# The end of a two-layer decode kernel: order of the closing products, the row layout of w_down, and the form of the last projection

## Chip, cores and metric

The kernel runs on one core of one Trainium2 chip. The metric is the time of one execution on the device in microseconds (us); the median of three runs of the kernel before is 651.43 us (650.32 to 651.67). One execution was recorded by the hardware profiler; all views below come from it.

## What is computed

Four sequences (B = 4) each take one decode step through two identical layers. A layer is a grouped-query attention block over a cache of 8192 positions, and then a gated feed-forward block, each with a layer norm ahead and a residual sum behind. Both layers use the same weights and the same caches. All arrays are bf16.

```python
def _A_ref(x, k_cache, v_cache, wq, wo):      # x (4,1,512); caches (4,8,8192,128)
    q = (x @ wq) ...                          # 32 query heads of 128, 4 for each of 8 cache heads
    scores = einsum(q, k) * 128 ** -0.5
    o = einsum(softmax(scores), v)
    return o.reshape(B, 1, 4096) @ wo

def _B_ref(x, w_gate, w_up, w_down):          # 512 -> 1792 -> 512
    return (silu(x @ w_gate) * (x @ w_up)) @ w_down

x = A_x
x = x + _A_ref(layernorm(x), ...);  x = x + _B_ref(layernorm(x), ...)
x = x + _A_ref(layernorm(x), ...);  x = x + _B_ref(layernorm(x), ...)
```

## The kernel before

**Units and slots.** The attention of a layer is cut into 16 units: a unit is one sequence and a pair of cache heads (its K is 4 MB, its V is 4 MB). Unit u belongs to head pair u // 4 and sequence u % 4. Layer 0 takes the units in the order 0 to 15; layer 1 takes 15, 14, 13 (which it partly finds still in SBUF) and then 0 to 12, so that unit 12 is the last. K and V go into four slots of SBUF and a fifth one that first held wq. The list `cmds` holds all transfers in order; `pump` issues the next one on the SP queue as soon as the pieces of the slot that it needs have been given back by `freed`. The V of a layer's last unit is loaded in three parts (blocks 0 to 3, 4 and 5, 6 and 7). The slot of an earlier K then takes the feed-forward weights: w_gate, the part of w_up that is not kept from layer 0, and w_down (`load_weight`, `load_wd`). The last part of w_down lies where the transposed probabilities of the last unit stood (`late_pT`), so it is issued only when those are used up.

**One unit.** `keys` transposes K on DVE (`turn`, L480) and multiplies it with the query on PE (`scores`, L504). Then come the steps of the softmax: `max_p` and `max_t` find the maximum, `exps` subtracts it and takes the exponential on ACT (L526, L529, L531, L533), `total` sums with a product with ones on PE and a reciprocal on DVE (L549, L552), and `turn_p` transposes the probabilities on DVE (L545). `values` multiplies them with V on PE in four parts (`products`, L604, in groups of four matmuls that write to four 32-row groups of the same bank), `gather` adds up eight or four sub-blocks on DVE (L656, L659), `combine` multiplies with a selection matrix on PE (L664) and scales with the reciprocal of the total (L666). When all four sequences of a head pair are done, `mix` reorders the result (L681, L684) and `project` multiplies it with a quarter of wo (L693).

**The order of the work** is written by hand. `blocks` is a list of PE blocks with an assumed time of 0.9 us each. `line` is a list of small steps with a gap, a tag and a function; `advance` takes the time of each block off the first step's gap and issues steps that are due. `flush(tag)` issues all steps up to the last one with that tag. Ahead of the second last unit's products (unit 11 in layer 1) all steps tagged with the last unit are flushed, that is also its exponential, total and transpose. In part 2 of the last unit (`part(2)`, L620 to L626) the steps left in the line except a projection are issued first, then the products of the second half of the positions on the first two blocks, then the gather of those; part 3 has the products on the other two blocks, the projection that was held back, the other half of the gather, and combine.

**The feed-forward block** (`ffn`, L760 to L808). `center` computes x minus its mean; 56 products with w_gate and 56 with w_up (L776, weights stationary, four columns moving) follow, with the norm's deviation in the middle of the first 56 (L725, L727, L729). L783 to L790 form silu(gate) * up, `hT`. Then 56 products with w_down (L795) in four parts. Row f of w_down must lie in the same partition as value f of hT. For a part of e rows per partition the row is a * 128 + p * e + (fo - a), so that gate and up weights are read at a step of e elements: four for fo = 0 to 11 and two for fo = 12 and 13. In layer 1 the sum with x goes to `xoT` (L805), four transposes (L849) in two pairs turn it, DVE and ACT copy one pair each to SBUF (L855, L857), and SP sends the result out (L859). The copy on DVE is recorded as a write of all names in `PB`, of which `xoT` is one.

The parts of w_down before:

```python
WD = ((0, 4), (4, 8), (8, 12), (12, 14))
```

Of the kernel before, what the change touches and what calls it, by code (L numbers as in the profile page):

```python
# [103 lines left out]
def bass_interleave_layers__gqa_block_cached__swiglu_ffn__decode_kernel(  # L104
# [40 lines left out]
    with ExitStack() as es:  # L145
# [11 lines left out]
        wq_sb = kv[:, QS, :].rearrange("p (k f) -> p k f", k=KT)  # L157
        WQ = [f"wq{i}" for i in range(2)]
        wo_sb = sb("wo_sb", [P, Hq, D], BF16)
        WD = ((0, 4), (4, 8), (8, 12), (12, 14))  # L160

        W_SLOT = (1, 3)
        O_WU = KT * F
# [5 lines left out]
            o = k // 2 * 2 * P + k % 2  # L169
            return slice(o, o + 2 * P - 1, 2)  # L170

        def columns(o, e=2):
            return kvf[:, o:o + e * (P - 1) + 1:e]

        def wg_at(s, k, f, e):
            return columns(s * SL + k * F + f, e)

        def wu_at(s, k, f, e):
            o = k * F + f
            return columns((NSLOT + 1) * SL + o if o < RES else s * SL + O_WU + o - RES, e)  # L180

        def wd_at(s, fo, k):
            return columns(s * SL + O_WD + fo * D + pick2(k).start)
# [37 lines left out]
        u0 += 3 * B  # L221
        xx, xc = (pbf[:, u0 + i * XB:u0 + (i + 1) * XB] for i in range(2))
        u0 += 2 * XB
        xoT = pb[:, 2 * u0:2 * u0 + XB]
        assert 2 * u0 + XB <= SW and SW >= D
        xio = pb[0:B, 0:D]
        PB = ["pb", "gr", "eg", "gw", "hT", "xs", "vs", "lnv", "xx", "xc", "xoT"]

        GP = G // 2
        RJ = [NA] * (GP - 1) + [2]  # L230
# [23 lines left out]
        def place(role, a, b, rows=slice(0, P)):  # L254
            k, o = (ONE, ROLE[role][1]) if held[0] else (ROLE[role][0], 0)
            assert o + b <= BANKF
            return bank(k)[rows, o + a:o + b], f"pb{k}"

        sem = lambda name: es.enter_context(nc.semaphore(name))
        engines = {"pe": nc.tensor, "act": nc.scalar, "dve": nc.vector, "pool": nc.gpsimd, "sp": nc.sync}  # L260
# [130 lines left out]

        def load_wd(w0, j, also=()):
            a, b = WD[j]
            T.dma("sp", w0[:, O_WD + a * D:O_WD + b * D],
                  B_w_down[a * P:b * P, :].rearrange("(p e) n -> p (e n)", e=b - a), sem_w["wd"][j],
                  writes=[f"wd{j}"] + list(also))

        def pump():
# [168 lines left out]
        def keys(L, u, before, lag):  # L567
            def block(q):
                if q == 0:
                    place_q(L, u)  # L570
                scores(L, u, q)
                finished(K(L, u), q, q + 1)
                if q == NB - 1:
                    step = lambda gap, fn: [gap, u, lambda: fn(u)]
                    line.extend([step(0.0, max_p), step(1.2, max_t)])
                    (line if before is None else behind.setdefault(before, [])).extend(
                        [step(0.9, exps), step(1.0, total), step(0.3, lambda u: turn_p(L, u))])

# [9 lines left out]
        def values(L, u):  # L588
# [21 lines left out]
            def part(i):  # L610
                if i == 0:
                    flush(order[L][-1] if u == order[L][-2] else u)
                h = i // 2
                ts = range(i % 2 * (TB // 2), (i % 2 + 1) * (TB // 2))
                if not last:
                    products(h, 0, QH, ts)
                elif not h:
                    products(h, 0, QH // 2, ts)
                    products(h, QH // 2, QH, ts)
                elif i == 2:  # L620
                    while line and line[0][1] != "proj":
                        line.pop(0)[2]()
                    for step in line:
                        step[0] = 99.0
                    products(h, 0, QH // 2, range(TB))
                    gather(0, QH // 2)  # L626
                else:
                    products(h, QH // 2, QH, range(TB))
                if i % 2:
                    finished(V(L, u), h * QH, (h + 1) * QH)  # L630
                if i == 3:
                    if p_name == "late":
                        freed(W_SLOT[L], NB, NB + 1)
# [126 lines left out]
        def ffn(L):  # L760
# [8 lines left out]
            for at, wname, bk in ((wg_at, "wg", gb), (wu_at, "wu", ub)):  # L769
                for fo in range(FO):  # L770
                    if bk == gb and fo == FO // 2:
                        deviation(zero_sb, "zero")
                    a, b = next(w for w in WD if w[0] <= fo < w[1])
                    f = a * P + fo - a
                    for kt in range(KT):
                        T.op("pe", lambda e: e.matmul(bank(bk)[:, fo * B:(fo + 1) * B],  # L776
                                                      lhsT=at(s, kt, f, b - a),
                                                      rhs=xn[:, kt * B:(kt + 1) * B],
                                                      start=(kt == 0), stop=(kt == KT - 1)),
                             reads=rooms[wname] + names[wname] + ["xn"], writes=[f"pb{bk}"],  # L780
                             sig=(fo == FO - 1 and kt == KT - 1))
                freed(s, *((0, 3) if wname == "wg" else (3, 4)))
# [5 lines left out]
            T.op("dve", lambda e: e.reciprocal(eg, eg), reads=["eg"], writes=["eg"])  # L788
            T.op("dve", lambda e: e.tensor_tensor(eg, gw, eg, ALU.mult), reads=["gw", "eg"], writes=["eg"])
            T.op("dve", lambda e: e.tensor_tensor(hT, eg, uT, ALU.mult), reads=[f"pb{ub}", "eg"], writes=["hT"])  # L790
            for j, (a, b) in enumerate(WD):
                k = OBK[0] if j else SBK[1]
                for nt in range(KT):
                    for fo in range(a, b):
                        T.op("pe", lambda e: e.matmul(bank(k)[:, nt * B:(nt + 1) * B],  # L795
                                                      lhsT=wd_at(s, fo, nt),
                                                      rhs=hT[:, fo * B:(fo + 1) * B],
                                                      start=(j < 2 and nt == 0 and fo == a),
                                                      stop=(j in (0, len(WD) - 1) and nt == KT - 1 and fo == b - 1)),
                             reads=["hT", f"wd{j}"] + rooms["wd"], writes=[f"pb{k}"], sig=(fo == b - 1))  # L800
                if not j:
                    add_to_x(bank(k)[:, 0:XB], f"pb{k}")
            freed(s, 4, NB)
            if L == 1:
                T.op("dve", lambda e: e.tensor_tensor(xoT, xT[:], bank(k)[:, 0:XB], ALU.add),  # L805
                     reads=["x", f"pb{k}"], writes=["xoT"])
            else:
                add_to_x(bank(k)[:, 0:XB], f"pb{k}")  # L808


        load_weight("wq", 0)
# [30 lines left out]
            ffn(L)  # L842
        assert issued[0] == len(cmds)

        for c, (k, eng) in enumerate(((LNB, "dve"), (OUTB, "act"))):
            ob = bank_bf(k)[0:B, 0:2 * P]
            for e_ in range(2):
                kt = 2 * c + e_
                T.op("pe", lambda e: e.matmul(ob[:, e_ * P:(e_ + 1) * P], lhsT=xoT[:, kt * B:(kt + 1) * B],  # L849
                                              rhs=ident, is_transpose=True, start=True, stop=True),  # L850
                     reads=["xoT", "ident"], writes=[f"pb{k}"], sig=(e_ == 1))
            to = xio[:, c * 2 * P:(c + 1) * 2 * P].rearrange("b (p e) -> b e p", e=2)
            src = ob.rearrange("b (e p) -> b e p", e=2)
            if eng == "dve":
                T.op("dve", lambda e: e.tensor_copy(to, src), reads=[f"pb{k}"], writes=PB)  # L855
            else:
                T.op("act", lambda e: e.activation(to, src, ACTF.Copy), reads=[f"pb{k}"], writes=["y1"])  # L857
        T.wait_res("sp", reads=["pb", "y1"])
        nc.sync.dma_start(out.rearrange("b s d -> (b s) d"), xio).then_inc(sem_out, 16)  # L859
        nc.sync.wait_ge(sem_out, 16)  # L860

# [27 lines left out]
```

## Time and profile before

| | |
|---|---|
| median of three runs | 651.43 us (650.32 to 651.67) |
| the profiled execution | 650.82 us |
| its span, first to last instruction | 648.9 us |
| mean granted TensorE clock | 0.834 of full speed |
| busy PE / PE weight loads / DVE / ACT | 430.7 / 187.4 / 422.9 / 39.0 us |
| moved by DMA | 273.41 MB, mean 421 GB/s |
| 28 loads of a whole K (4096 KB), issue to landing | median 32.0 us |
| 27 loads of a whole V (4096 KB), issue to landing | median 36.3 us |
| output DMA issued | at 647.36 us |

A line of the timeline reads: start in us from the start of the span, busy time in us, engine, line of the kernel, operation, out<-in tiles, sizes, number of instructions, and in brackets how long the engine had been idle and what it waited for. PE is the matrix engine, PEld its weight load, DVE the vector engine, ACT the scalar engine, SP the queue that issues the DMAs. A line of the view by stretches has the stretch, then busy time and number of instructions for each engine, the granted clock, the busy share of the DMA engines and what they moved in GB/s. A busy time of several matmuls runs from the first start to the last end; the start to start distance of two neighbours is their pace.

### The profile page before, as it was taken

To read this page: it belongs to the slowest core of one execution; us is meant where nothing else is said; L and a number is where in the kernel's file an instruction comes from. 1 tells how busy PE (TensorE), PEld (TensorE's weight loads), DVE (VectorE), ACT (ScalarE), POOL (GpSimd) and SP (SyncE) were. 2 spreads that over 40 slices of the span, in tenths; PEclk is the share of its full clock that TensorE was granted. 3 is DMA by queue.
4 is the path that set the end of the run, shared out by engine and by line. 5 is a ranking of instruction groups with operands and counts; after the bars stand their busy time and mean duration, and the time that the engine had idled before them with its cause. 6 is when DMAs were issued, how large, how long until landed. Compare 5 with 4: busy or idle time off the path is not lost.

```text
span 648.9 us, 7943 instructions
## 1 busy us (share of the span) xinstructions
PE 430.7 (66%) x3344; PEld 187.4 (29%) x3344; DVE 422.9 (65%) x704; ACT 39.0 (6%) x108; POOL 11.1 (2%) x43
## 2 busy tenths in 40 slices
PE   2584467465775655766757888857656568665866
PEld 2231122122332222223237332222222123322235
DVE  1585467466786656777842879967766667766943
ACT  1000000000000000000010000000000000000010
POOL 0000000000000000000000000000000000000000
PEclk9996887699877788968965899998777887777966
DMA  8999999999999999999999999999999999999995
GB/s 364 441 422 419 447 423 422 427 438 425 433 435 424 437 431 420 443 425 423 437 411 400 413 435 429 437 428 428 437 427 430 431 430 435 426 431 434 426 416 209
DMA packets 14035, 273.41 MB, mean 421 GB/s; under 512 B 1448, under 2 KB 1456, under 8 KB 4912
## 3 DMA queue, kind: packets, MB, share of 16 engines
q1 hardware_dynamic: 14000, 272.91, 98.6%
q8 instruction: 26, 0.43, 0.3%
q14 instruction: 9, 0.07, 0.0%
HBM read 272.90 MB, written 0.00 MB: 421 GB/s over the span
## 4 chain that ended last, share of the span: by engine, by line
DMA 54%; DVE 30%; PE 9%; issue 4%; another core or an unknown queue 1%; SPq 1%; ACT 1%; DVEq 0%; ACTq 0%
DMA kvf<-in_A_k_cache_dram 51%; DVE kvf L480 21%; DMA kvf<-in_B_w_down_dram 3%; PE ps L604 3%; DVE pT L545 3%; DVE pb L659 3%; PE ps L504 2%; SPq L93 1%; DVE pb L656 1%; PE ps L776 1%; PE ps L738 1%; PE ps L795 0%; ACT pb L531 0%; PE ps L515 0%
## 5 line engine op out<-in xcount | busy, mean ns | idle before, releaser
L504 PE MATMUL ps<-kvf,zq 128*128 128x512 bf16 x1024 | 300.3, 435 | 167.3 <-DVE kvf L480 162.9
L480 DVE STREAM_TRANSPOSE kvf<-kvf 128x1024 f32<-128x1024 f32 x246 | 290.3, 1216 | 135.1 <-DMA kvf<-in_A_k_cache_dram 134.9
L504 PEld LDWEIGHTS ps<-kvf,zq 128*128 128x128 bf16 x1024 | 95.1, 108 | 321.5 <-DVE kvf L480 222.9
L604 PE MATMUL ps<-kvf,pT 128*32 128x512 bf16 x960 | 65.8, 398 | 7.0 <-DVE pT L545 7.0
L531 ACT ACTIVATE pb<-ps,tiny 128x512 bf16<-128x512 f32 x32 | 22.0, 687 | 550.5 <-DVE tiny L529 388.2
L545 DVE STREAM_TRANSPOSE pT<-pb 64x512 bf16<-64x512 bf16 x60 | 40.9, 682 | 1.0
L659 DVE SCALAR_TENSOR_TENSOR pb<-ps,tiny,pb 128x128 f32<-128x128 f32 x96 | 33.7, 351 | 3.5
L604 PEld LDWEIGHTS ps<-kvf,pT 128*32 128x32 bf16 x960 | 21.9, 98 | 36.2 <-issue 20.9
L510 DVE TENSOR_REDUCE tiny<-ps 128x1 f32<-128x512 f32 x32 | 21.9, 686 | 5.1 <-PE ps L504 4.5
L664 PEld LDWEIGHTS ps<-sel,pb 128*128 128x128 f32 x64 | 16.4, 269 | 18.6 <-DVE pb L659 10.7
L518 DVE TENSOR_REDUCE m<-ps 1x8 f32<-1x128 f32 x32 | 8.8, 275 | 17.8 <-PE ps L515 17.8
L549 PE MATMUL ps<-rsm,tiny 128*128 128x8 f32 x64 | 12.3, 264 | 10.6 <-ACT rsm L533 10.5
L494 POOL TENSOR_TENSOR zq<-scr,tiny 128x64 bf16<-128x64 bf16 x30 | 8.9, 298 | 562.0 <-PE ps L504 562.0
L549 PEld LDWEIGHTS ps<-rsm,tiny 128*128 128x128 f32 x64 | 10.9, 202 | 21.8 <-ACT rsm L533 20.5
L664 PE MATMUL ps<-sel,pb 128*128 128x8 f32 x64 | 12.5, 269 | 6.7 <-DVE pb L659 6.7
L526 PEld LDWEIGHTS ps<-m,tiny 1*128 1x128 f32 x64 | 10.4, 203 | 16.4 <-issue 13.8
L656 DVE TENSOR_SCALAR pb<-ps,tiny 128x128 f32<-128x128 f32 x32 | 10.1, 317 | 6.1 <-PE ps L604 6.1
L526 PE MATMUL ps<-m,tiny 1*128 1x8 f32 x64 | 13.3, 278 | 0.9 <-DVE rl L552 0.3
L552 DVE RECIPROCAL rl<-ps 128x8 f32<-128x8 f32 x32 | 5.6, 176 | 9.7 <-PE ps L549 9.7
L693 PE MATMUL ps<-oT,wo_sb 128*128 128x4 bf16 x256 | 7.7, 165 | 3.8 <-DVE oT L684 3.8
L738 PE MATMUL ps<-xn,kvf 128*128 128x4 bf16 x256 | 7.6, 166 | 3.7 <-DMA kvf<-in_A_wq_dram 2.9
L533 ACT ACTIVATE rsm<-head,tiny 128x8 f32<-128x8 f32 x32 | 9.6, 301 | 1.0
(72 smaller groups left out, 121.9 us busy)
## 6 DMA issues: line engine op xcount, KB each, us to landing
kvf<-in_A_k_cache_dram SPq DMA_DIRECT2D x28, 4096.0 KB, 32.0
kvf<-in_A_v_cache_dram SPq DMA_DIRECT2D x27, 4096.0 KB, 36.3
kvf<-in_A_v_cache_dram SPq DMA_DIRECT2D x4, 2048.0 KB, 19.1
kvf<-in_A_k_cache_dram SPq DMA_DIRECT2D x4, 2048.0 KB, 9.9
kvf<-in_A_wq_dram SPq DMA_DIRECT2D x2, 2048.0 KB, 9.7
wo_sb<-in_A_wo_dram SPq DMA_DIRECT2D x4, 1024.0 KB, 41.7
kvf<-in_A_v_cache_dram SPq DMA_DIRECT2D x4, 1024.0 KB, 34.5
kvf<-in_B_w_gate_dram SPq DMA_DIRECT2D x2, 1792.0 KB, 24.9
```

The source lines that it names most:

```text
L480: T.op("dve", lambda e: e.transpose(w, w), reads=[f"s{s}.{q}"], writes=[f"s{s}.{q}"])
L504: T.op("pe", lambda e: e.matmul(bank(bk)[:, 0:SW], lhsT=zq[:, z0:z0 + P], rhs=w[:, :, c // 2, :, c % 2], start=(q == 0 and c == 0), stop=( ...
L510: T.op("dve", lambda e: e.tensor_reduce(mx[:], bank(bk)[:, 0:SW], AX.X, ALU.max), reads=[f"pb{bk}"], writes=["mx"])
L526: T.op("pe", lambda e: e.matmul(at, lhsT=onesf[0:1, :].to_broadcast([1, P]), rhs=m8[:, turn_of[u], :], start=True, stop=True), reads=[f"m8 ...
L531: T.op("act", lambda e: e.activation(pb[:], bank(bk)[:, 0:SW], ACTF.Exp, bias=nm, accum_out=rs), reads=[f"pb{bk}", "nm"], writes=PB + ["rs"])
L545: T.op("dve", lambda e: e.transpose(dst, pb[hp]), reads=["pb"], writes=[name])
L549: T.op("pe", lambda e: e.matmul(at, lhsT=ones, rhs=rsm[:], start=True, stop=True), reads=["rsm", "onesf"], writes=[name])
L604: T.op("pe", lambda e: e.matmul(bank(k)[j * QB:(j + 1) * QB, q0 * Dh:q1 * Dh], lhsT=p_t[:, t, h, :], rhs=v[:, q0:q1, t, :], start=(h == 0 ...
L656: T.op("dve", lambda e: e.tensor_scalar(acc, o, own[:, 0:1], None, op0=ALU.mult), reads=[f"pb{k}", "own"], writes=PB)
L659: T.op("dve", lambda e: e.scalar_tensor_tensor(acc, o, own[:, q:q + 1], acc, op0=ALU.mult, op1=ALU.add), reads=[f"pb{k}", "own", "pb"], wr ...
L664: T.op("pe", lambda e: e.matmul(at, lhsT=acc, rhs=sel[:], start=True, stop=True), reads=["pb", "sel"], writes=[name])
L738: T.op("pe", lambda e: e.matmul(at[:, h * B:(h + 1) * B], lhsT=wq_sb[:, kt, h * Dh:(h + 1) * Dh], rhs=xn[:, kt * B:(kt + 1) * B], start=(k ...
```

## The change

It has four parts. In part 2 of the last unit the products come ahead of the steps that are left in the line. The last unit's total comes after its transpose, with a gap of 2.5 us in the line and no tag, so that it is not flushed ahead of unit 11's products. w_down is loaded in three parts instead of four, all with two rows per partition side by side (chunks of 2 KB), so that gate and up weights are read at a step of two throughout. And in layer 1 the last projection has hT stationary (four columns) and w_down moving (128 columns), in four column groups that write four quarters of the output directly in row form; x is added by eight float32 products with the identity that write every second column of a quarter; four copies, two on DVE and two on ACT, bring the quarters to SBUF.

```diff
-        WD = ((0, 4), (4, 8), (8, 12), (12, 14))
+        WD = ((0, 6), (6, 12), (12, 14))
...
-        def columns(o, e=2):
-            return kvf[:, o:o + e * (P - 1) + 1:e]
+        def columns(o):
+            return kvf[:, o:o + 2 * P - 1:2]
...
+        def quarter(j):
+            return bank(STEP)[j * QB:j * QB + B, 0:P]
...
-            T.dma("sp", w0[:, O_WD + a * D:O_WD + b * D],
-                  B_w_down[a * P:b * P, :].rearrange("(p e) n -> p (e n)", e=b - a), sem_w["wd"][j],
+            T.dma("sp", w0[:, O_WD + a * D:O_WD + b * D].rearrange("p (m x) -> p m x", x=2 * D),
+                  B_w_down[a * P:b * P, :].rearrange("(m p e) n -> p m (e n)", p=P, e=2), sem_w["wd"][j],
...
-                    (line if before is None else behind.setdefault(before, [])).extend(
-                        [step(0.9, exps), step(1.0, total), step(0.3, lambda u: turn_p(L, u))])
+                    after = [step(0.9, exps), step(1.0, total), step(0.3, lambda u: turn_p(L, u))]
+                    if u == order[L][-1]:
+                        after = [after[0], after[2], [2.5, None, lambda: total(u)]]
+                    (line if before is None else behind.setdefault(before, [])).extend(after)
...
                 elif i == 2:
+                    products(h, 0, QH // 2, range(TB))
                     while line and line[0][1] != "proj":
                         line.pop(0)[2]()
                     for step in line:
                         step[0] = 99.0
-                    products(h, 0, QH // 2, range(TB))
                     gather(0, QH // 2)
...
-                    a, b = next(w for w in WD if w[0] <= fo < w[1])
-                    f = a * P + fo - a
+                    f = fo // 2 * 2 * P + fo % 2
...
+            if L == 1:
+                for i, (a, b) in enumerate(WD):
+                    for fo in range(a, b):
+                        for j in range(NA):
+                            o = s * SL + O_WD + fo * D + j * P
+                            T.op("pe", lambda e: e.matmul(quarter(j), lhsT=hT[:, fo * B:(fo + 1) * B],
+                                                          rhs=kvf[:, o:o + P], start=(fo == 0), stop=(fo == FO - 1)),
+                                 reads=["hT", f"wd{i}"] + rooms["wd"], writes=[f"pb{STEP}"],
+                                 sig=(fo == b - 1 and j == NA - 1))
+                    if i:
+                        continue
+                    for kt in range(KT):
+                        for m in range(2):
+                            o = m * (P // 2)
+                            T.op("pe", lambda e: e.matmul(quarter(kt // 2 * 2 + m)[:, kt % 2::2],
+                                                          lhsT=xT[:, kt * B:(kt + 1) * B], rhs=identf[:, o:o + P // 2],
+                                                          start=False, stop=False),
+                                 reads=["x", "ident"], writes=[f"pb{STEP}"], sig=(kt == KT - 1 and m == 1))
+                freed(s, 4, NB)
+                return
...
-        for c, (k, eng) in enumerate(((LNB, "dve"), (OUTB, "act"))):
-            ob = bank_bf(k)[0:B, 0:2 * P]
-            for e_ in range(2):
-                kt = 2 * c + e_
-                T.op("pe", lambda e: e.matmul(ob[:, e_ * P:(e_ + 1) * P], lhsT=xoT[:, kt * B:(kt + 1) * B],
-                                              rhs=ident, is_transpose=True, start=True, stop=True),
-                     reads=["xoT", "ident"], writes=[f"pb{k}"], sig=(e_ == 1))
...
+        for j in range(NA):
+            to = xio[:, j * P:(j + 1) * P]
+            if j % 2:
+                T.op("act", lambda e: e.activation(to, quarter(j), ACTF.Copy), reads=[f"pb{STEP}"], writes=[f"y{j}"])
             else:
-                T.op("act", lambda e: e.activation(to, src, ACTF.Copy), reads=[f"pb{k}"], writes=["y1"])
-        T.wait_res("sp", reads=["pb", "y1"])
+                T.op("dve", lambda e: e.tensor_copy(to, quarter(j)), reads=[f"pb{STEP}"], writes=[f"y{j}"])
+        T.wait_res("sp", reads=[f"y{j}" for j in range(NA)])
```

More of the change, by code (lines that the diff above doesn't have):

```diff
@@ L170, in pick2, with wg_at, wu_at @@
             return slice(o, o + 2 * P - 1, 2)
-        def columns(o, e=2):
-            return kvf[:, o:o + e * (P - 1) + 1:e]
-        def wg_at(s, k, f, e):
-            return columns(s * SL + k * F + f, e)
-        def wu_at(s, k, f, e):
+        def columns(o):
+            return kvf[:, o:o + 2 * P - 1:2]
+        def wg_at(s, k, f):
+            return columns(s * SL + k * F + f)
+        def wu_at(s, k, f):
             o = k * F + f
-            return columns((NSLOT + 1) * SL + o if o < RES else s * SL + O_WU + o - RES, e)
+            return columns((NSLOT + 1) * SL + o if o < RES else s * SL + O_WU + o - RES)
         def wd_at(s, fo, k):
@@ L223, in bass_interleave_layers__gqa_block_cached__swiglu_ffn__decode_kernel @@
         u0 += 2 * XB
-        xoT = pb[:, 2 * u0:2 * u0 + XB]
-        assert 2 * u0 + XB <= SW and SW >= D
+        assert 2 * u0 <= SW and SW >= D and KT == NA == 4
         xio = pb[0:B, 0:D]
-        PB = ["pb", "gr", "eg", "gw", "hT", "xs", "vs", "lnv", "xx", "xc", "xoT"]
+        PB = ["pb", "gr", "eg", "gw", "hT", "xs", "vs", "lnv", "xx", "xc"]
         GP = G // 2
@@ L772, in ffn @@
                         deviation(zero_sb, "zero")
-                    a, b = next(w for w in WD if w[0] <= fo < w[1])
-                    f = a * P + fo - a
+                    f = fo // 2 * 2 * P + fo % 2
                     for kt in range(KT):
                         T.op("pe", lambda e: e.matmul(bank(bk)[:, fo * B:(fo + 1) * B],
-                                                      lhsT=at(s, kt, f, b - a),
+                                                      lhsT=at(s, kt, f),
                                                       rhs=xn[:, kt * B:(kt + 1) * B],
@@ L803, in ffn @@
             freed(s, 4, NB)
[L804 to L808, printed above, removed]
+            add_to_x(bank(k)[:, 0:XB], f"pb{k}")
         load_weight("wq", 0)
@@ L843, in bass_interleave_layers__gqa_block_cached__swiglu_ffn__decode_kernel @@
         assert issued[0] == len(cmds)
-        for c, (k, eng) in enumerate(((LNB, "dve"), (OUTB, "act"))):
-            ob = bank_bf(k)[0:B, 0:2 * P]
-            for e_ in range(2):
-                kt = 2 * c + e_
-                T.op("pe", lambda e: e.matmul(ob[:, e_ * P:(e_ + 1) * P], lhsT=xoT[:, kt * B:(kt + 1) * B],
-                                              rhs=ident, is_transpose=True, start=True, stop=True),
-                     reads=["xoT", "ident"], writes=[f"pb{k}"], sig=(e_ == 1))
[L852 to L855, printed above, removed]
-            else:
-                T.op("act", lambda e: e.activation(to, src, ACTF.Copy), reads=[f"pb{k}"], writes=["y1"])
-        T.wait_res("sp", reads=["pb", "y1"])
+        for j in range(NA):
+            to = xio[:, j * P:(j + 1) * P]
+            if j % 2:
+                T.op("act", lambda e: e.activation(to, quarter(j), ACTF.Copy), reads=[f"pb{STEP}"], writes=[f"y{j}"])
+            else:
+                T.op("dve", lambda e: e.tensor_copy(to, quarter(j)), reads=[f"pb{STEP}"], writes=[f"y{j}"])
+        T.wait_res("sp", reads=[f"y{j}" for j in range(NA)])
         nc.sync.dma_start(out.rearrange("b s d -> (b s) d"), xio).then_inc(sem_out, 16)
```

## The prediction, made before the changed kernel was run

> **What bounds the kernel now.** I read the page first. Its table of slices has the DMA row near 9 until the last slice, so the weight and cache stream sets the pace; only what follows its end can gain.
>
> ```profile
> DMA  8999999999999999999999999999999999999995
> GB/s 364 441 422 419 447 423 422 427 438 425 433 435 424 437 431 420 443 425 423 437 411 400 413 435 429 437 428 428 437 427 430 431 430 435 426 431 434 426 416 209
> ```
>
> Next the DMA issues with their time to landing, one by one. The last unit's V comes in three parts, issued at 587.47, 588.61 and 588.99 us, landing 40.6, 41.9 and 44.0 us later: at 628.1, 630.5 and **633.0**. By the same sums w_gate lands at 637.4, the rest of w_up at 638.7, and the four parts of w_down at 640.8, 642.0, 643.3 and **643.9**. So two clocks run in the tail: no last product before 633.0, no last projection before 643.9. Then the timeline of the end:
>
> ```profile
> 632.89 0.42 PE L681 MATMUL ps<-oT,identf 128*32 128x8 bf16 x16 [0.27 <-DVE oT L666]
> 633.15 1.05 PE L604 MATMUL ps<-kvf 128*32 128x256 bf16 x32
> 633.81 0.35 DVE L656 TENSOR_SCALAR pb<-ps,tiny 128x128 f32<-128x128 f32 x1 [0.27 <-PE ps L604]
> 634.19 1.19 DVE L659 SCALAR_TENSOR_TENSOR pb<-ps,tiny,pb 128x128 f32<-128x128 f32 x3
> 635.44 0.39 PE L664 MATMUL ps<-sel,pb 128*128 128x8 f32 x2 [0.35 <-DVE pb L659]
> ...
> 643.55 1.65 PE L795 MATMUL ps<-pb,kvf 128*128 128x4 bf16 x56 [0.31 <-DVE pb L790]
> ...
> 645.31 0.17 DVE L805 TENSOR_TENSOR pb<-xT,ps 128x16 bf16<-128x16 f32 x1 [0.97 <-PE ps L795]
> 645.54 0.38 PE L849 MATMUL ps<-identf,pb 128*4 128x128 bf16 x2 [0.33 <-DVE pb L805]
> 645.95 0.43 DVE L855 COPY pb<-ps 4x256 bf16<-4x256 bf16 x1 [0.47 <-PE ps L849]
> 646.44 0.37 PE L849 MATMUL ps<-identf,pb 128*4 128x128 bf16 x2 [0.52 <-DVE pb L855]
> 646.85 0.44 ACT L857 ACTIVATE pb<-ps 4x256 bf16<-4x256 bf16 x1 [4.87 <-PE ps L849]
> 647.36 0.29 SPq L859 DMA_DIRECT2D out_dram<-pb  x1
> ```
>
> All 32 products of the second half start together at 633.15, behind the mix of L681, although half their V landed at 630.5. And from the last L795 product (end 645.20) to the output's issue 2.16 us pass in series, the second pair of L849 waiting for a DVE copy that only shares a name with it. After the last landing PE, DVE and ACT take turns; nothing else is in flight.
>
> **The change, part by part.** Times on the trace's axis; the issue of the output at 647.36 is what must move.
>
> *Third part's products ahead.* They now follow the previous unit's combine and wait for no mix. They could run from 630.5 on; before, PE got to them at 633.15. With the later total (below), the first 16 and the two accumulations on them are over by some 633.3: L604 of unit 11 starts at 625.1 instead of 627.0, takes 3.6 plus 0.5 for the total, the first half of unit 12 ends at 630.7 and its gather (0.35 + 3 x 0.39) with it, combine, 16 products, mix and cast end near 632.5, two accumulations follow. The other 16 wait for 633.0: they issue in 0.50 us (half of L604's 1.05), DVE gets the result 0.16 later (633.65 to 633.81 in the rows), two accumulations take 0.39 each. Combine starts at 634.5 instead of 635.44: **0.9 gained**. The projection held back (32 products, 0.96) lies beside these accumulations. Mix and its cast now queue behind a wait for V, but their reader is the late projection.
>
> *Last total later.* Two passes of L549 (0.52) leave the path ahead of unit 11's products; its reciprocal (0.21) falls into DVE time idle for 2.0 us, and turn_p moves ahead of it by 1.1. Worth nothing by itself after 633.0; it makes the above possible.
>
> *w_down with step two.* Two effects. First, gate and up weights are read at every second element in place of every fourth for 96 of 112 products of L776. The old row shows both steps in one line, the busy-time view of L776 in four stretches:
>
> ```profile
> 640.41:641.08 0.67, 0.66 (x20) 0.50 0.59 237
> 641.08:641.29 0.21, 0.21 (x13) 0.50 0.69 276
> ```
>
> Twenty products in 0.67 (33 ns each) are step four; the second stretch lies on the step-two ones, 27 ns each in the trace's starts. 96 x 6.7 ns = 0.64; half of it comes before L783, and the DVE steps L783 to L789 (1.52) then end beside the up products, so **0.6 gained**. The Trainium skill ("SBUF — State Buffer", section on the DMA port swizzle) says a read may stride over 8 bf16 elements free of charge within a 16-byte line; by it step four costs nothing, and the sum would be 1.0 instead of 1.6. The trace disagrees, 33 against 27 ns at the same granted clock of 0.50; I follow the trace (rival 4).
>
> Second, SP issues 896 rows of w_down for 512: 768 of 2 KB instead of 384 of 4 KB, plus the 128 of the tail. In the packet records a 2 KB row takes 84 ns, a 4 KB one 163, so each of 16 engines loses 24 x 5 ns = 0.14 per layer: V lands 0.14 later and the last w_down 0.28 later (644.2; the part before it 643.5). **0.14 lost** on the path. SP already stands 9.4 and 6.0 us in the old second and third issue (full queue); with 384 more rows the second ends near 633 and the tail part about 635.5, 8 us before their data can flow: hidden. If SP stood longer than that, every microsecond would come out at the end.
>
> In layer 0 the same edits end at w_down's landing, with several us of K queued behind: no effect.
>
> *Last projection in four column groups.* Still 56 products, in 14 groups of four with 128 columns. Groups of four in L604 take 0.213 for 256 columns at clock 0.50, so 0.107 here, 27 ns each: L795's pace; no change but 0.11 more for the last to stream. Added: 8 float32 products with the identity, two passes each, between the first and second w_down part. No row shows them. From below, 16 passes at 27 ns: 0.43. From above, 8 one after another at the 0.59 that two passes take in L710: 4.7. The nearest row is L515 (float32, one pass, 128 columns, next product 0.20 later at full clock): 0.10 to 0.20 a pass of 64 columns at half clock, and neighbours go to two column groups, so half of 16 passes count: 0.8 to 1.6. I take **1.0 lost**. Only a wait for the second part could hide it, and that has landed by then.
>
> Removed: L805, four L849, L855 and L857. Added: four copies of 128 columns, two on DVE and two on ACT side by side. L855 and L684 give 1.07 ns an element on DVE, 0.29 a copy; L857 and L785 0.95 on ACT, 0.32 a copy: 0.6 for two in a row. Tail: 0.05 + 0.11 + 0.6 + 0.07 = 0.83 instead of 2.16: **1.3 gained**. add_to_x after the first part was beside other work.
>
> *Clock.* The slices show 1.00 from 631.1 to 638.0, then 0.50. With products thinned out of the slice from 631.1, it may fall to 0.50 at 634.5; combine and projection then take 0.3 more (L664 0.39 against L710 0.59), and L710 no longer saves 0.2 by being earlier. I take **0.1 lost**. The term may differ from run to run.
>
> **Sum**: 0.9 + 0.6 - 0.14 - 1.0 + 1.3 - 0.1 = 1.6. The profiled execution took 650.82 (span 648.9 and 1.9 around it), which gives 649.2. It stands 0.6 below the median 651.43, so for the median I forecast **649.8**. About 0.2% (1.3 us) can be told from no change.
>
> **Rivals.**
> 1. *The weights' end takes over.* If the identity products cost 0.4, the second w_down part (643.5) and the last (644.2) bind: 644.2 + 0.21 + 0.83 = 645.2, 2.1 gained, 649.3. For it: only 0.5 us lie between. Against: eight float32 products at the issue floor. Chance 0.13.
> 2. *The identity products are the new bound (slower).* They write every second PSUM column in float32. At 0.59 each, unoverlapped, the first w_down part ends at 643.0, they at 647.7, the rest (0.85) and tail (0.83) bring 649.4: 2.0 late, 653.5. It decides from 0.33 us per product (2.6 in all). The Trainium skill ("SBUF — State Buffer", same section) says a non-contiguous PSUM pattern slows matmuls markedly, which is this mechanism; no row here shows its size. Chance 0.12.
> 3. *The reorder brings nothing*: combine still comes at 635.4, because PE's earlier work slips behind 633.0 or the clock falls. Then 1.6 - 0.9 + 0.1 = 0.8, 650.6. For it: DVE has only some 0.4 us to spare. Chance 0.2.
> 4. *The step of the weights is worth nothing*: 1.6 - 0.6 = 1.0, 650.4, if what made the first 96 products slower was something other than their step. Against: layer 0's L776 shows the same two paces at the same place. By the skill's rule above this would be so. Chance 0.03.
> The forecast's mechanism (gain 1.0 to 2.2) has 0.52.
>
> **Chances.** Of the forecast three quarters pass 1.3, rival 1 does, rivals 3 and 4 mostly not: faster 0.53; within 0.2% 0.33; slower 0.14 (rival 2 and the spread of the stream). Range: from 2.7 gained to 0.5 lost, 648.7 to 651.9; it leaves out rival 2 and little else.
>
> **What would show it.** Right: the last 16 products of L604 at 633.2 alone, combine by 634.9, all gate products 27 ns apart, identity products about 1.0 us together, output issued 0.9 after the last product, at 645.5 to 646.3. Wrong: SP in a w_down issue past 640, a PE wait for DMA inside the last projection, or identity products of 0.3 us each.

## The result, and the profile after

The changed kernel takes 649.46 us (median of 22 runs, 648.59 to 650.91), the kernel before 650.69 us (22 runs beside it, 649.92 to 652.97). The ratio, worked out over all runs, is **0.9977, with a 95% interval of 0.9970 to 0.9983**: 1.5 us faster (1.1 to 2.0); the two medians alone lie 1.2 us apart. 1.6 us were forecast. The sum came out right partly by luck: its largest gain but one, the order of the last unit, was taken far too large, and other terms made up for it.

The end of the changed kernel in the timeline (weight loads left out; L608 are the products, L663 the gather, L668 combine, L779 the gate and up products, L799 the last projection, L808 the identity products, L867 and L869 the copies):

```profile
631.73 0.62 PE L608 MATMUL ps<-kvf 128*32 128x256 bf16 x16 [0.40 <-DMA kvf<-in_A_v_cache_dram]
...
634.22 0.62 PE L608 MATMUL ps<-kvf 128*32 128x256 bf16 x16 [1.69 <-DMA kvf<-in_A_v_cache_dram]
...
634.90 0.74 DVE L663 SCALAR_TENSOR_TENSOR pb<-ps,tiny,pb 128x128 f32<-128x128 f32 x2 [1.47 <-PE ps L608]
...
635.69 0.39 PE L668 MATMUL ps<-sel,pb 128*128 128x8 f32 x2
...
643.34 0.81 PE L799 MATMUL ps<-kvf,pb 128*4 128x128 bf16 x24 [0.43 <-DVE pb L793]
...
643.93 0.64 PE L808 MATMUL ps<-identf,xT 128*4 128x64 f32 x16
...
644.36 1.07 PE L799 MATMUL ps<-kvf,pb 128*4 128x128 bf16 x32
645.49 0.56 ACT L867 ACTIVATE pb<-ps 4x128 bf16<-4x128 f32 x2 [3.53 <-PE ps L799]
645.49 0.60 DVE L869 CAST pb<-ps 4x128 bf16<-4x128 f32 x2 [2.20 <-PE ps L799]
646.12 0.29 SPq L871 DMA_DIRECT2D out_dram<-pb  x1
```

The first 16 products now run at 631.7, ahead of the last landing, and the other 16 stand alone, 1.69 us behind a wait for V. The output is issued 0.69 us after the last product's end (645.43) instead of 2.15. The identity products start at 643.93, and the next part at 644.36: 0.43 us for all 16 passes.

From the two profiles, stage by stage (us; a plus is time saved):

| stage | before | after | forecast | measured |
|---|---|---|---|---|
| landing of the last V part | 633.02 | 634.18 | -0.14 | -1.16 |
| to the start of the last combine | 2.42 | 1.51 | +0.9 | +0.91 |
| to the first gate product | 3.63 | 3.67 | -0.1 | -0.04 |
| to the first w_down product | 4.48 | 3.98 | +0.6 | +0.50 |
| to the end of the last one | 1.66 | 2.09 | -1.0 | -0.43 |
| to the issue of the output | 2.15 | 0.69 | +1.3 | +1.46 |

The first two rows are one thing: V landed later in this execution, and how much of the 0.91 is real depends on that. The two profiles alone can't tell. Every landing below is read off the one profiled execution of its kernel.

### The profile page after: what moved, and what is told of

Read it like the earlier page. It is cut to its first block, busy times and chain, and to the rows that moved or that the text cites. A ratio compares the mean times of both kernels' runs of the same rounds, so it can differ in the third digit from the quotient of the medians.

```text
span 647.7 us, 7963 instructions
## 1 busy us (share of the span) xinstructions
PE 429.5 (66%) x3356; PEld 185.2 (29%) x3356; DVE 422.7 (65%) x703; ACT 39.1 (6%) x109; POOL 11.1 (2%) x43
## 2 busy tenths in 40 slices
DMA packets 14771, 273.41 MB, mean 422 GB/s; under 512 B 1416, under 2 KB 1424, under 8 KB 5648
## 4 chain that ended last, share of the span: by engine, by line
DMA 61%; DVE 24%; PE 9%; issue 3%; another core or an unknown queue 1%; SPq 1%; ACT 0%; DVEq 0%; ACTq 0%
DMA kvf<-in_A_k_cache_dram 51%; DVE kvf L482 18%; DMA kvf<-in_A_v_cache_dram 7%; PE ps L506 4%; DMA kvf<-in_B_w_down_dram 4%; DVE pT L547 2%; PE ps L608 2%; DVE pb L663 2%; SPq L93 1%; PE ps L742 1%; DVE pb L660 0%; DVE kvf L447 0%; PE ps L517 0%; PE ps L697 0%
## 5 line engine op out<-in xcount | busy, mean ns | idle before, releaser
L608 PE MATMUL ps<-kvf,pT 128*32 128x512 bf16 x960 | 67.1, 402 | 9.2 <-DVE pT L547 9.2
L663 DVE SCALAR_TENSOR_TENSOR pb<-ps,tiny,pb 128x128 f32<-128x128 f32 x96 | 33.7, 351 | 5.4 <-PE ps L608 2.1
L608 PEld LDWEIGHTS ps<-kvf,pT 128*32 128x32 bf16 x960 | 21.9, 98 | 37.6 <-issue 22.6
L668 PEld LDWEIGHTS ps<-sel,pb 128*128 128x128 f32 x64 | 16.7, 274 | 18.0 <-DVE pb L663 10.1
L668 PE MATMUL ps<-sel,pb 128*128 128x8 f32 x64 | 12.9, 274 | 6.2 <-DVE pb L663 6.2
```

Of the source, the lines that this page charges most:

```text
L608: T.op("pe", lambda e: e.matmul(bank(k)[j * QB:(j + 1) * QB, q0 * Dh:q1 * Dh], lhsT=p_t[:, t, h, :], rhs=v[:, q0:q1, t, :], start=(h == 0 ...
L663: T.op("dve", lambda e: e.scalar_tensor_tensor(acc, o, own[:, q:q + 1], acc, op0=ALU.mult, op1=ALU.add), reads=[f"pb{k}", "own", "pb"], wr ...
L668: T.op("pe", lambda e: e.matmul(at, lhsT=acc, rhs=sel[:], start=True, stop=True), reads=["pb", "sel"], writes=[name])
```

## The experiments

Theory at the outset: the terms add up, the order of the last unit among them. Rival: the last V part binds in most runs, the order is worth nothing, and the closing form carries the gain.

**e1_only_tail**: the kernel before with the new last projection alone.

```diff
+            if L == 1:
+                for i, (a, b) in enumerate(WD):
...
-        for c, (k, eng) in enumerate(((LNB, "dve"), (OUTB, "act"))):
...
+        for j in range(NA):
+            to = xio[:, j * P:(j + 1) * P]
...
```

> The kernel before with the last projection of the change alone (four column groups, identity products, four copies). Theory (the terms add up): from the end of the last w_down product to the output's issue 0.7 us instead of 2.16, the projection itself 2.1 instead of 1.65 for the identity products (0.43 in the changed kernel's trace); so about 1.0 us less than before, ratio 0.9985. Rival (the closing form carries the whole gain): 1.4 to 1.5 us less, ratio 0.9977, as the full change.

649.5 against 650.64 us, ratio 0.9986 (0.9976 to 0.9995): 0.9 us, as the sum of its two stages (2.09 and 0.69 again). The interval just takes in the 0.9977 of the rival, so it is the stages of the trace, not the time, that speak for the theory. But its profile holds more. It has the **old** order, and still:

```profile
633.75 0.35 DVE L661 SCALAR_TENSOR_TENSOR pb<-ps,tiny,pb 128x128 f32<-128x128 f32 x1
634.46 0.62 PE L606 MATMUL ps<-kvf 128*32 128x256 bf16 x16 [1.15 <-DMA kvf<-in_A_v_cache_dram]
...
635.92 0.39 PE L666 MATMUL ps<-sel,pb 128*128 128x8 f32 x2
```

The first 16 products and their two accumulations were through by 634.1, and the other 16 waited 1.15 us for V, which landed at 634.41. Combine starts 1.51 us behind the landing, exactly as in the changed kernel. In this run the reorder had nothing to gain.

**e2_only_front**: the kernel before with the two edits of the order alone.

```diff
+                    if u == order[L][-1]:
+                        after = [after[0], after[2], [2.5, None, lambda: total(u)]]
...
+                    products(h, 0, QH // 2, range(TB))
                     while line and line[0][1] != "proj":
...
-                    products(h, 0, QH // 2, range(TB))
```

> The kernel before with the last unit's order alone (third part's products ahead, last total later). Theory: from the landing of the last V part to the start of the last combine 1.5 us instead of 2.42, the rest unchanged; about 0.9 us less than before, ratio 0.9986. Rival (the landing binds and the reorder brings nothing): landing to combine shrinks but the feed-forward weights or the clock take it back; within 0.3 us of before, ratio 1.000.

650.82 against 650.64 us, ratio 1.0009 (1.0000 to 1.0018). The rival held: no gain, and rather a small loss (0.6 us, 0 to 1.2). Its profiled execution is one of the longer ones (652.08 us) and shows how a loss comes about. In the timeline of the same place, and in the view by stretches (columns from PEclk on: granted clock, DMA share, GB/s):

```profile
634.63 1.04 PE L606 MATMUL ps<-kvf 128*32 128x256 bf16 x16 [1.67 <-DMA kvf<-in_A_v_cache_dram]
...
636.52 0.60 PE L666 MATMUL ps<-sel,pb 128*128 128x8 f32 x2
```

```profile
632.00:636.00 4.00, 2.17 (x62) 1.56 (x63) 1.07 (x4) 0.00 (x0) 0.00 (x0) 0.82 1.00 411
636.00:640.00 4.00, 2.96 (x64) 2.67 (x61) 1.32 (x7) 0.00 (x0) 0.00 (x0) 0.50 0.96 379
```

PE, done with everything else, stood idle ahead of V; the granted clock went to 0.50 at 634.5, and the 16 products took 1.04 us instead of 0.62, combine 0.60 instead of 0.39. Landing to combine is 1.93 us.

**e3_only_step**: the kernel before with w_down in three parts at step two alone.

```diff
-        WD = ((0, 4), (4, 8), (8, 12), (12, 14))
+        WD = ((0, 6), (6, 12), (12, 14))
-            return kvf[:, o:o + e * (P - 1) + 1:e]
+            return kvf[:, o:o + 2 * P - 1:2]
```

> The kernel before with w_down in three parts and step two alone. Theory: all 112 gate and up products of layer 1 27 ns apart, first of them to first w_down product 4.0 us instead of 4.49; the 2 KB rows cost 0.14 us per layer in the stream; about 0.35 us less than before, ratio 0.9995. Rival (the smaller rows cost more than the step gains): the last w_down part lands a microsecond later against the last V part than before (10.9 us) and the time is 0.3 to 1 us longer.

650.12 against 650.64 us, ratio 0.9995 (0.9986 to 1.0004): the expected 0.35 us lies inside, but the time alone can't tell it from nothing. The trace can: first gate product to first w_down product is 3.98 us instead of 4.49. In w_down's landings, from the end of w_up to the last part, the kernels with 4 KB rows e1, e2 and e4 show 4.37 to 4.38 us (before: 5.24), those with 2 KB rows 4.38 to 4.91.

**e4_no_false_wait**: the kernel before, with the copy on DVE recorded under its own name.

```diff
-                T.op("dve", lambda e: e.tensor_copy(to, src), reads=[f"pb{k}"], writes=PB)
+                T.op("dve", lambda e: e.tensor_copy(to, src), reads=[f"pb{k}"], writes=["y0"])
...
-        T.wait_res("sp", reads=["pb", "y1"])
+        T.wait_res("sp", reads=["y0", "y1"])
```

> The kernel before, where the copy on DVE is recorded under a name of its own, so that the second pair of transposes waits for no copy. Nothing else changes. Theory: the second pair follows the first within 0.15 us and both copies run side by side; last w_down product to output issue 1.3 us instead of 2.16; about 0.85 us less than before, ratio 0.9987, so that most of what the new last projection brings is to be had without it. Rival (the copies were the long part, or DVE and ACT disturb each other): under 0.4 us less.

650.06 against 650.64 us, ratio 0.9990 (0.9981 to 0.9999). Last product to output 1.47 us instead of 2.15, so 0.68 rather than 0.85: all four transposes (L849) now run together, 0.59 us, and ACT's copy follows at 646.38:

```profile
645.76 0.59 PE L849 MATMUL ps<-identf,pb 128*4 128x128 bf16 x4 [0.33 <-DVE pb L805]
646.17 0.43 DVE L855 COPY pb<-ps 4x256 bf16<-4x256 bf16 x1 [0.47 <-PE ps L849]
646.38 0.44 ACT L857 ACTIVATE pb<-ps 4x256 bf16<-4x256 bf16 x1 [4.20 <-PE ps L849]
646.90 0.29 SPq L859 DMA_DIRECT2D out_dram<-pb  x1
```

Two names edited bring 0.68 of the 1.03 us that the whole new closing form brings (1.46 less 0.43), by these stages; the time of the whole says 0.6 (0.1 to 1.2).

This run also shows how far the landing wanders. Up to its last copies it issues the same work as the kernel before, and yet its last V part, the second of these two transfers, landed at 634.16 instead of 633.02:

```profile
L93 SPq DMA_DIRECT2D kvf<-in_A_v_cache_dram x2: 328/377/426, 588.8 to 589.1; - x2
DMA to landing us min/median/max: 42.0/43.5/45.0
```

**e5_total_early** and **e6_mix_ahead**: the changed kernel with one of the two edits of the order taken back, the total in e5 (first diff), the place of the products in e6 (second).

```diff
-                    if u == order[L][-1]:
-                        after = [after[0], after[2], [2.5, None, lambda: total(u)]]
```

```diff
-                    products(h, 0, QH // 2, range(TB))
                     while line and line[0][1] != "proj":
...
+                    products(h, 0, QH // 2, range(TB))
```

> The changed kernel with the last unit's total back ahead of unit 11's products; the products ahead of the mix stay. Theory: the total holds unit 11's products back by some 2 us, the whole row up to the second accumulation slips past the last V part, and landing to combine grows from 1.5 to about 2.0 us; 0.4 to 0.7 us more than the changed kernel. Rival (the products ahead of the mix do it alone): no difference, within 0.2 us.

> The changed kernel with the steps left in the line (mix of the head pair) ahead of the third part's products again; the total stays late. Theory: with the late total the mix is over 1.5 us before the last V part lands, so its place no longer matters; within 0.2 us of the changed kernel. Rival (the order of products and mix is what gains): 0.5 us or more slower than the changed kernel.

Against 650.9 us before: 648.85 us, ratio 0.9971 (0.9959 to 0.9982), and 649.19 us, ratio 0.9975 (0.9965 to 0.9985). Neither can be told from the changed kernel's 0.9977. Landing to combine is 1.51 us in both. The theory failed on e5, which should have been slower. Its two accumulations were over at 634.03, V had landed at 633.80, and the second accumulations began at 634.52: there were some 0.5 us to spare. In these two executions either of the two edits was enough by itself.

**e7_no_identity** and **e8_identity_first**: the identity products left out (the lines with a minus), and in e8 put ahead of all w_down products (those with a plus).

```diff
+                for kt in (0, 2, 1, 3):
+                    for m in range(2):
...
+                                                      start=(kt % 2 == 0), stop=False),
...
                 for i, (a, b) in enumerate(WD):
...
-                    for kt in range(KT):
-                        for m in range(2):
```

> The changed kernel without the eight identity products; this leaves the sum with x out of the output. Theory: they cost 0.43 us on the path (16 passes, four at a time, 0.107 each four); first to last w_down product 1.55 instead of 1.78 plus 0.3, the time 0.4 us less than the changed kernel if the second w_down part is there, and no less than the landing of the last part plus 0.9. Rival (the wait for w_down's parts takes their place): a wait for DMA appears in the projection and the time stays within 0.15 us.

> The changed kernel with the identity products ahead of all w_down products, where PE waits for hT (idle 0.43 us in the changed kernel's trace). Theory: they are hidden there, first w_down product to last end 1.65 instead of 2.09, the time 0.4 us less than the changed kernel, ratio to the kernel before 0.997, unless the last w_down part (644.4 in that trace) comes too late. Rival (DMA takes over): a wait of PE for w_down of 0.3 us or more, and no gain beyond 0.15.

648.80 us, ratio 0.9972 (0.9961 to 0.9983), and 648.86 us, ratio 0.9970 (0.9958 to 0.9982). Without the identity products PE waits for w_down in their place, here 0.5 us, as the rival said; whether the time is 0.4 us shorter or the same, the ratio can't tell. The landing of the last part is then 1.12 us ahead of the output. At the head they vanish into the wait for hT, and the projection takes 1.66 us from first to last end, without a wait for DMA. First the timeline of e7, then of e8:

```profile
642.40 0.81 PE L799 MATMUL ps<-kvf,pb 128*4 128x128 bf16 x24 [0.43 <-DVE pb L793]
...
643.66 1.02 PE L799 MATMUL ps<-kvf,pb 128*4 128x128 bf16 x32 [0.46 <-DMA kvf<-in_B_w_down_dram]
```

```profile
643.78 0.61 PE L798 MATMUL ps<-identf,xT 128*4 128x64 f32 x16
644.01 0.21 DVE L793 TENSOR_TENSOR pb<-pb,ps 128x56 bf16<-128x56 f32 x1
...
644.28 1.66 PE L806 MATMUL ps<-kvf,pb 128*4 128x128 bf16 x56
```

The 0.43 us are seen in the trace of e8; in its ratio they can't be told from the changed kernel's.

**e9_old_front** and **e10_old_front_identity_first**: the changed kernel with both edits of the order taken back, and the same with e8's edit (diffs as in e2 and e8, the former backwards).

> The changed kernel with both edits of the last unit's order taken back: step two and the new last projection alone. Theory now (the last V part lands so late that the old order is through with its other work by then): landing to combine stays 1.51 us, the time is that of the changed kernel within 0.3 us, ratio to the kernel before 0.997 to 0.998. Rival (the reorder is worth the 0.9 us of the forecast in most runs): 0.9 us slower than the changed kernel, ratio 0.999.

> As the run before it, and the identity products ahead of all w_down products. Theory: landing of the last V to the output's issue 11.5 us instead of the changed kernel's 11.94, as the 0.43 us of identity products lie in PE's wait for hT; ratio to the kernel before about 0.997, the fastest of all. Rival (w_down's landing takes over): PE waits for DMA in the projection, landing of the last w_down part to output 1.1 us, no faster than the changed kernel.

Against 650.41 us before: 649.61 us, ratio 0.9984 (0.9975 to 0.9993), and 648.79 us, ratio 0.9979 (0.9971 to 0.9988). The former lies between the theory's 0.997 to 0.998 and the rival's 0.999. The theory's 1.51 us failed in its profile, the one case with the whole stream, beside the first, in which the old order bound: V landed at 633.33, combine started 2.01 us later. In e10 V landed at 633.74, combine came 1.54 us later, and the landing to the output took 11.54 us, as expected (changed kernel 11.94). It was expected to be the fastest of all, but its ratio can't be told from the changed kernel's.

**e11_early_v_before** and **e12_early_v_front**: the kernel before and e2, where the second last V is all but left out of the stream.

```diff
+            e = a * BW + 64 if it == V(1, order[1][-2]) else b * BW
-            T.dma("sp", kv[:, s, a * BW:b * BW], src[:, a * BW:b * BW], sm,
+            T.dma("sp", kv[:, s, a * BW:e], src[:, a * BW:e], sm,
```

> The kernel before, of whose second last V (unit 11 in layer 1) only the first 64 of 32768 elements of each row are loaded; this leaves most of that unit's values wrong. The last V then lands some 9.5 us earlier and can bind nothing. Theory: the tail is now set by PE and DVE alone, last combine at about 635.4 as in the profile before, however early V lands, and the next run shows what the order is worth. Rival: the chain itself moves earlier with the landings, so that the last V, not the order of the work, bound it all along.

> As the run before it, with the two edits of the last unit's order. Theory: where no landing binds, the order is worth what the forecast said or more: last combine 0.9 to 1.3 us earlier than in the run before it, the time 0.8 to 1.3 us shorter. Rival (the order is worth nothing anywhere, since it only moves waits among PE and DVE): combine and time within 0.3 us of that run.

Against 650.41 us: 650.51 us, ratio 0.9999 (0.9990 to 1.0008), and 648.58 us, ratio 0.9976 (0.9964 to 0.9987). Taking 4 MB out of the stream, so that the last V lands at 624.1, gains **nothing** with the old order. With the new one the ratio says 1.6 us (0.8 to 2.3), and the median is 1.9 us below e11's. Combine came at 636.6 in e11, not at the expected 635.4, because `max_t` came 1.15 us later in that execution. From the transpose of unit 12's maximum (`max_t`, which follows its scores) to the last combine, in the timelines of e11 and of e12:

```profile
618.84 0.27 PE L516 MATMUL ps<-identf,tiny 128*1 128x128 f32 x1
...
636.61 0.39 PE L665 MATMUL ps<-sel,pb 128*128 128x8 f32 x2 [0.35 <-DVE pb L660]
```

```profile
617.67 0.27 PE L516 MATMUL ps<-identf,tiny 128*1 128x128 f32 x1
...
632.92 0.39 PE L667 MATMUL ps<-sel,pb 128*128 128x8 f32 x2 [0.44 <-DVE pb L662]
```

17.77 us against 15.25. Where no landing binds, the two differ by 2.5 us, about twice what I expected; the theory's mechanism is there. Not all of it is the order itself. The full clock came back at 627.4 in e12, at 633.9 in e11 and at 629.3 in the changed kernel. From the first product of unit 11 to its combine, the same work in the same order, e12 (first line, view by stretches) took 0.64 us less than the changed kernel (second line), whose stretch no landing bound either:

```profile
624.78:630.01 5.23, 4.49 (x66) 2.13 (x66) 3.08 (x9) 1.08 (x3) 0.00 (x0) 0.75 0.93 371
625.07:630.94 5.87, 5.15 (x66) 2.42 (x66) 3.08 (x9) 1.08 (x3) 0.00 (x0) 0.64 0.99 412
```

So some 0.6 us of the 2.5 belong to the clock. Whether the new order itself brought the clock back sooner was not shown.

## Why the prediction was right, point by point

**The order of the last unit, "0.9 gained": the mechanism right, the size read off one execution.** The runs give a simple rule for the old order: combine starts 1.51 us after the last V part lands, or 17.75 us after max_t, whichever is later. It meets the seven profiles with the old order to 0.1 us (us from the start of the span):

| run | max_t | V landed | combine | by the rule |
|---|---|---|---|---|
| before | 617.69 | 633.02 | 635.44 | 635.44 |
| e1 | 617.80 | 634.41 | 635.92 | 635.92 |
| e3 | 617.41 | 633.68 | 635.19 | 635.19 |
| e4 | 617.99 | 634.16 | 635.67 | 635.74 |
| e9 | 617.69 | 633.33 | 635.34 | 635.44 |
| e10 | 617.59 | 633.74 | 635.27 | 635.34 |
| e11 | 618.84 | 624.14 | 636.61 | 636.59 |

The 17.75 is clearly the later one in three of them alone (before, e9, e11), and with another course of the clock it could be another number. What the reorder saves is the excess of the second over the first: 0.91 us in the profile before, where V landed at 633.02, the earliest of the full-stream kernels, 0.5 in e9, and 0 to 0.1 in e1, e3, e4 and e10. V's last part landed anywhere from 633.0 to 634.6 us in the twelve kernels with a full stream. So the term should, by this estimate, have been about 0.25 (the mean of these six), and the forecast read a draw as a constant: e4 shows that the landing moves by a microsecond with the same work ahead of it. The step that failed is the sentence "Combine starts at 634.5 instead of 635.44". Rival 3 (nothing from the reorder, chance 0.2) was nearly the truth for this part, with another reason than I gave: not PE slipping past the landing, but the landing coming later than PE. Its second reason, the falling clock, was seen in e2 and e8.

**Clock, "0.1 lost".** In the changed kernel it fell to 0.50 at 636.1 instead of 638.0, at a cost of 0.04 us. But in e2 and e8, both with the new order, it fell before the last products (634.5 and 633.3), for 0.4 us up to combine and 0.2 more to the first gate product. In the six profiles with the whole stream and the new order, or one half of it, it fell between 633.3 and 637.8, in the six with the old order between 635.6 and 638.4. With a gain of 0.25 in the mean and such losses in some runs, e2's ratio of 1.0009 is what remains. That the idle wait ahead of V lets the clock fall fits these traces; that it is the whole of e2's loss is not shown.

**Last projection, "1.0 lost" for the identity products: too much.** 0.43, the lower bound that I gave. The four passes of two neighbouring products started within 20 ns of each other, and the next four 0.107 us later; they were not pairs one after another. Rival 2 had no part. The Trainium skill ("SBUF — State Buffer", section on the DMA port swizzle) expects matmuls to slow on non-contiguous PSUM patterns. These write every second column and took 27 ns a pass, the pace of L795, so no such slowdown is seen here. One that hides behind this pace would not be seen, and a version that writes whole runs was not tried.

**Closing copies, "1.3 gained": 1.46.** The two copies on each engine took 0.56 and 0.60 us as reckoned (0.6). The column groups' last product ended later, as reckoned, but that time is counted in the row above.

**Step of the weights, "0.6 gained": 0.50.** The pace is as forecast. In the view of L779 alone, 22 products in the first stretch that held step-four ones before:

```profile
640.51:641.10 0.59, 0.56 (x22) 0.50 0.63 243
641.10:641.31 0.21, 0.21 (x14) 0.50 0.60 234
```

A product counts in every stretch that it overlaps, so the pace is not the stretch divided by the count; the starts lie 27 ns apart in both stretches, at the same clock of 0.50. The missing 0.1 is DVE: L793 now waits for L792, not for PE. Rival 4 falls: the same products took 33 ns each while they were read at a step of four. By the rule of the Trainium skill ("SBUF — State Buffer", section on the DMA port swizzle) a step of four would cost nothing. These traces disagree, and the measurement decides.

**Rows of 2 KB, "0.14 lost": rather 0.2.** In the changed kernel's packet records a row of 2 KB takes 85 ns and one of 4 KB 161. Two of the former replace one of the latter, 24 times per engine and layer: 24 x (2 x 85 - 161) ns = 0.22 us. The forecast had 5 ns where this has 9, and its 24 x 5 ns is 0.12, not 0.14. w_down took 4.4 to 4.9 us to land instead of mostly 4.4. SP's second issue stood 17.2 us (to 624.2, not to 633). That a full queue held it there is not shown; in e11, with 4 MB less in the stream, the two long issues stood 3.0 and 2.0 us instead of 9.4 and 6.0, which would fit. The tail part was issued at 634.9 and landed with the rest: hidden, as forecast. The page shows the rows as packets, 5648 under 8 KB where it had 4912:

```profile
DMA packets 14771, 273.41 MB, mean 422 GB/s; under 512 B 1416, under 2 KB 1424, under 8 KB 5648
```

**The sum.** Without the order's term the measured stages give 0.50 - 0.43 + 1.46 - 0.04 = 1.49, less 0.2 for the rows: 1.3. With 0.25 for the order it is 1.5, and the ratio says 1.5 (1.1 to 2.0). The forecast of 1.6 had 0.65 too much for the order and 0.1 too much for the step, and took some 0.1 too little off for the rows. Against that it took 0.57 too much off for the identity products and had 0.16 too little for the copies. That these nearly cancel is luck. Of the signs named ahead, the last 16 products alone and the output at 646.12 came as told. Combine came at 635.69 instead of by 634.9, as V landed later, and the identity products took 0.43 us instead of about 1.0. Rival 1 (w_down's landing takes over) is the next bound. In e7 it binds, with the output 1.12 us behind the last landing; in the changed kernel, e5, e6 and e9 the output is 1.4 to 1.75 us behind it, so 0.3 to 0.6 us are left.

What stays open: whether the reorder is worth a few tenths or nothing in the changed kernel. The intervals of e5, e6, e8, e9 and e10 all overlap.

## What to carry to other kernels

Where a wait for DMA and a chain of engines end within a microsecond of each other, take the landing from several executions before a gain is read off one: here its spread (633.0 to 634.6) was wider than the gain. A probe that takes the transfer out of the stream prices the chain alone; compare the granted clock of its two runs before the whole difference is given to the order. And look at a closing stretch for a wait that only a shared name makes: two names edited brought, by the stages of the traces, two thirds of what a new form of the projection brought.

## What the runs showed of the hardware beyond what was expected

Float32 products with four stationary columns, two passes each, in two neighbouring column groups started four passes at a time at clock 0.50: 16 of 64 columns in 0.43 us. Weights read at every fourth bf16 element load at 33 ns a product, at every second at 27 ns, clock 0.50 in both. The last of the 16 parts of V's final transfer came 0.05 to 1.16 us after the 15th in the kernels with the whole stream. A 16 KB packet of the instruction queue lasts 0.93 to 1.13 us in the records of the kernel before and the changed one. That would be enough to make such a gap, but that it does was not shown; the packet nearest ahead began at 629.1 where the gap was largest (e8) and at 628.9 where it was smallest (e2).
